# A 31st key/value slot in a one-core, two-layer cached-attention decode kernel

## The chip, the cores and the metric

The kernel runs on one core of a Trainium2 chip. The metric is the device time of one execution in microseconds; the time before is the median of three runs.

## What is computed

Eight sequences decode one token each through two identical layers; a layer is an attention block over a cache (A) and a mixer/MLP block (B), both with residuals. With one token per sequence the mixer's shifted parts fall away, so B is `x1 = x`, then `x1 + gelu(LN(x1) @ w3) @ w4`.

```python
def _A_ref(x, k_cache, v_cache, wq, wo):          # x (8, 1, 448), caches (8, 8, 4096, 256) bf16
    q = (x @ wq).reshape(B, 1, 16, 256)...
    k = jnp.repeat(k_cache, 2, axis=1)            # 16 query heads, 8 key/value heads
    v = jnp.repeat(v_cache, 2, axis=1)
    scores = jnp.einsum("bhqd,bhkd->bhqk", q, k) * (256 ** -0.5)
    o = jnp.einsum("bhqk,bhkd->bhqd", _softmax(scores), v)
    return o.reshape(B, 1, 4096) @ wo
...
x = x + _A_ref(_layernorm(x), A_k_cache, A_v_cache, A_wq, A_wo)
x = x + _B_ref(_layernorm(x), B_w1, B_w2, B_w3, B_w4)
x = x + _A_ref(...)                               # the same caches and weights again
x = x + _B_ref(...)
```

## The kernel before, in words

**Units of work.** A batch has 8 key/value heads, treated as four pairs m = 0..3. A head's 4096 x 256 keys (or values) are four chunks of 512 KB: 128 partitions x 2048 bf16, eight consecutive keys a partition. A chunk lies in one of `NSLOT = 30` slots of `SLOT = 2048` columns. One load brings one, two or four neighbouring slots (512, 1024 or 2048 KB); all loads are issued by SP (line 444), in one order fixed beforehand.

**Layers.** The batches run one after another, each with its layer-0 pairs, then a *turn*, then its layer-1 pairs. Layer 1 reads the same keys: those of pairs 1, 2 and 3 stay in slots in transposed form (24 chunks, of which three are *parked* as transposed tiles in PSUM and copied back by ACT, `unpark`, line 1100), and pair 0's keys are loaded again. V is loaded for both layers. In the stream, the loads of one pair's K alternate with those of the V of the pair before.

**Scores.** A chunk of K is transposed in one of two ways. The first `NN[m]` chunks of a head go whole through PE (128 x 128, line 819) into PSUM and are evicted by ACT into the same slot (line 878); their scores need the plain query (line 888, 16 matmuls a chunk). The others are transposed by DVE in 32 x 32 blocks into another free slot (line 900, two instructions a chunk, some 1.2 us each), and the raw slot comes free; their scores need the query spread into a block diagonal (`diagonal`, lines 623, 629, 635, kept in `qe`) and come from line 909, 16 matmuls a chunk as well.

**Softmax of a pair** (`kpart`): maximum over DVE (923) and POOL (925), subtraction (927), exponential by ACT into a tile `pE` (930), POOL's copy of the natural columns into `pN` (932), a PE transpose of `pE` (936), a DVE transpose into `pT` with zeros between the columns (938), then the sum (941), POOL's all-reduce (943) and the reciprocal (944). `pT` and `pN` have four buffers each; the zeros are written once at the start.

**P*V** (`vpart`): mostly with V moving, 128 x 512 (line 1002). The result in PSUM is split into two bf16 parts, the negated rounding by ACT (1012) and the remainder by DVE (1014), in a tile `half`, and eight small matmuls gather it (1023). The last pair before a turn has V as the stationary operand instead (974), which needs no such parts.

**The turn** (`turn`): output projection (1051), residual, norm, w3, gelu, w4 (592), norm, wq as rows (667), an ACT copy of the rows into `qe` (671), a transposition into columns (675), and the block diagonals of pairs 1, 2, 3 and 0.

**The planner** (`Plan.schedule`) runs when the program is built: every operation has an engine, a cost, dependences and a priority, and a list scheduler fixes the order on each engine and the slot of each load. An ACT or DVE operation that makes a chunk (an operation with a `target`) takes a free slot when it is placed. A load of four or two slots is cut in half when no such run of slots is free and the stream would run dry:

```python
if short and len(us) == 4 and transfer < t + DRY4:
    order.insert(nxt[0] + 1, self.split(u, users))
...
if (len(us) == 2 and short and transfer < t + DRY and one is not None and ...):
    order.insert(nxt[0] + 1, self.split(u, users))
```

## Time and profile before

| | |
|---|---|
| median of three runs | 1101.11 us (1100.97 to 1103.56) |
| the profiled execution | 1103.15 us, span 1101.3 us |
| busy: PE, PEld, DVE, ACT, POOL | 775.3, 534.9, 792.4, 223.4, 77.5 us |
| loads into slots | 361 (85 of 2 MB, 217 of 1 MB, 58 of 512 KB, one small) |

PE is TensorE's matmuls, PEld its weight loads, which overlap them; DVE is VectorE, ACT ScalarE, POOL GpSimd, SP SyncE, which only issues loads. A group's line gives line, engine, operation, tiles, shapes and count, then busy us and mean ns of one, then the idle time before them with what ended it. `A <- B` among the waits reads "A waited for B". A stretch's line gives its length, each engine's busy time (with the number of instructions), the granted TensorE clock, the DMA engines' share and GB/s.

### The profile page before, as it was taken

To read this page: it belongs to the slowest core of one execution; us is meant where nothing else is said; L and a number is where in the kernel's file an instruction comes from. 1 tells how busy PE (TensorE), PEld (TensorE's weight loads), DVE (VectorE), ACT (ScalarE), POOL (GpSimd) and SP (SyncE) were. 2 spreads that over 40 slices of the span, in tenths; PEclk is the share of its full clock that TensorE was granted. 3 is DMA by queue.
4 is the path that set the end of the run, shared out by engine and by line. 5 is a ranking of instruction groups with operands and counts; after the bars stand their busy time and mean duration, and the time that the engine had idled before them with its cause. 6 is when DMAs were issued, how large, how long until landed. Compare 5 with 4: busy or idle time off the path is not lost.

```text
span 1101.3 us, 33772 instructions
## 1 busy us (share of the span) xinstructions
PE 775.3 (70%) x15552; PEld 534.9 (49%) x15552; DVE 792.4 (72%) x1472; ACT 223.4 (20%) x313; POOL 77.5 (7%) x208
## 2 busy tenths in 40 slices
PE   2567588668757875778757787577776688676874
PEld 2355455354545563555525554354644456345553
DVE  4999549864897379955898558974689737995552
ACT  1022122112211131213202132121221113121310
POOL 0000001000100010000100000000010001000010
PEclk9999565565655555555655555555555555555555
DMA  9999999999999999999999999999999999999994
GB/s 342 406 421 405 395 392 423 423 394 410 425 425 408 412 425 427 423 397 415 424 427 420 399 420 427 426 418 405 414 427 423 406 408 423 428 422 395 420 425 182
DMA packets 59166, 448.96 MB, mean 408 GB/s; under 512 B 6016, under 2 KB 12048, under 8 KB 19984
## 3 DMA queue, kind: packets, MB, share of 16 engines
q1 hardware_dynamic: 59024, 446.80, 98.4%
q8 instruction: 122, 2.00, 0.7%
q14 instruction: 20, 0.16, 0.0%
HBM read 446.77 MB, written 0.01 MB: 406 GB/s over the span
## 4 chain that ended last, share of the span: by engine, by line
DMA 37%; DVE 28%; PE 20%; issue 7%; ACT 4%; POOL 1%; POOLq 0%; ACTq 0%; DVEq 0%; SPq 0%
DMA slot<-in_A_k_cache_dram 26%; DVE slot L900 18%; DMA slot<-in_A_v_cache_dram 11%; PE psV L1002 7%; PE psS L909 7%; ACT slot L1100 3%; PE psS L888 2%; DVE pT L938 1%; PE psT L592 1%; DVE half L1014 1%; PE psT L1051 1%; ACT half L1012 1%; DVE small L527 1%; PE psK L819 1%; POOL small L555 1%
## 5 line engine op out<-in xcount | busy, mean ns | idle before, releaser
L900 DVE STREAM_TRANSPOSE slot<-slot 128x1024 bf16<-128x1024 bf16 x512 | 602.5, 1220 | 49.1 <-DMA slot<-in_A_k_cache_dram 48.4
L909 PE MATMUL psS<-qe,slot 128*128 128x8 bf16 x6528 | 257.8, 175 | 164.5 <-DVE slot L900 140.5
L909 PEld LDWEIGHTS psS<-qe,slot 128*128 128x128 bf16 x6528 | 218.9, 105 | 291.9 <-DVE slot L900 236.3
L1002 PE MATMUL psV<-slot,pT 128*8 128x512 bf16 x1416 | 178.9, 582 | 6.6 <-DMA slot<-in_A_v_cache_dram 3.7
L878 ACT COPY slot<-psK 128x1024 bf16<-128x1024 bf16 x112 | 109.7, 1023 | 182.2 <-PE psK L819 182.2
L819 PE MATMUL psK<-ident,slot 128*128 128x128 bf16 x896 | 102.5, 302 | 15.3 <-DMA slot<-in_A_k_cache_dram 9.4
L1012 ACT ACTIVATE half<-psV 128x512 bf16<-128x512 f32 x55 | 33.0, 600 | 318.5 <-PE psV L1002 303.7
L819 PEld LDWEIGHTS psK<-ident,slot 128*128 128x128 bf16 x896 | 86.5, 140 | 20.3 <-DMA slot<-in_A_k_cache_dram 10.4
L1014 DVE TENSOR_TENSOR half<-psV,half 128x512 bf16<-128x512 f32 x55 | 37.3, 678 | 61.3 <-ACT half L1012 61.1
L925 POOL PARTITION_ALL_REDUCE small<-small x64 | 23.9, 374 | 699.0 <-DVE small L923 699.0
L938 DVE STREAM_TRANSPOSE pT<-psS 128x128 bf16<-128x128 bf16 x64 | 44.8, 701 | 8.8 <-PE psS L936 8.3
L1002 PE MATMUL psV<-slot,pN 128*8 128x512 bf16 x344 | 46.7, 553 | 2.9 <-DMA slot<-in_A_v_cache_dram 2.8
L930 ACT ACTIVATE pE<-psS 128x128 bf16<-128x128 f32 x64 | 18.3, 286 | 133.3 <-DVE psS L927 121.5
L977 DVE TENSOR_REDUCE small<-psV 128x8 f32<-128x32 f32 x9 | 1.7, 192 | 56.1 <-PE psV L974 56.1
L888 PE MATMUL psS<-small,slot 128*128 128x2 bf16 x896 | 31.4, 166 | 11.1 <-ACT slot L1100 6.4
L1002 PEld LDWEIGHTS psV<-slot,pT 128*8 128x8 bf16 x1416 | 25.9, 88 | 25.0 <-issue 11.0
L1051 PE MATMUL psT<-small,wo_sb 128*128 128x1 bf16 x1024 | 32.8, 165 | 7.4 <-DVE small L980 3.9
L888 PE MATMUL psS<-qo,slot 128*128 128x2 bf16 x768 | 27.9, 167 | 12.8 <-ACT slot L878 7.4
L974 PE MATMUL psV<-pT,slot 128*128 128x2 bf16 x864 | 28.8, 166 | 11.0 <-DMA slot<-in_A_v_cache_dram 10.9
L888 PEld LDWEIGHTS psS<-qo,slot 128*128 128x128 bf16 x768 | 24.0, 102 | 25.5 <-ACT slot L878 18.1
L888 PEld LDWEIGHTS psS<-small,slot 128*128 128x128 bf16 x896 | 28.1, 104 | 16.2 <-ACT slot L1100 8.5
L923 DVE TENSOR_REDUCE small<-psS 128x4 f32<-128x128 f32 x64 | 17.8, 278 | 23.8 <-PE psS L909 23.6
(156 smaller groups left out, 681.2 us busy)
## 6 DMA issues: line engine op xcount, KB each, us to landing
slot<-in_A_v_cache_dram SPq DMA_DIRECT2D x151, 1024.0 KB, 9.7
slot<-in_A_k_cache_dram SPq DMA_DIRECT2D x43, 2048.0 KB, 19.3
slot<-in_A_v_cache_dram SPq DMA_DIRECT2D x42, 2048.0 KB, 22.5
slot<-in_A_k_cache_dram SPq DMA_DIRECT2D x66, 1024.0 KB, 12.3
slot<-in_A_v_cache_dram SPq DMA_DIRECT2D x42, 512.0 KB, 6.6
slot<-in_A_k_cache_dram SPq DMA_DIRECT2D x16, 512.0 KB, 6.1
wo_sb<-in_A_wo_dram SPq DMA_DIRECT2D x4, 896.0 KB, 19.0
wq_sb<-in_A_wq_dram SPq DMA_DIRECT2D x3, 1024.0 KB, 9.5
```

Of the source, the lines that this page charges most:

```text
L819: last = e.transpose(tile[:, j * P:(j + 1) * P], slots[u.slot][:, o:o + P], ident[:, :])
L878: return e.copy(slots[u.slot][:, 1024 * t:1024 * t + 1024], tile)
L888: last = e.matmul(o, slots[u.slot][:, i:i + P], q, start=(cc == 0), stop=(cc == 1))
L900: return e.transpose(o, i)
L909: last = e.matmul(o, slots[u.slot][:, i:i + P], qe[:, 128 * pm_ + 64 * s + 8 * g:128 * pm_ + 64 * s + 8 * g + 8], start=(g == 0), stop=(g ...
L938: add("dve", lambda e: e.transpose(pT[y].rearrange("p (n u r) -> p n r u", u=3, r=4)[:, :, :, 0:3:2], psS[x][:, 128:192].bitcast(bf).rearr ...
L974: last = e.matmul(o, slots[u.slot][:, i:i + P], w, start=(j == 0), stop=(j == 7))
L1002: last = e.matmul(psV[x][32 * i:32 * i + 8, :].rearrange("p (k d) -> p k d", k=2), w, v, start=(s == 0 and c == 0), stop=(s == 1 and c == ...
L1012: add("act", lambda e: e.activation(part(0), psV[x][:, :], ACT.Copy, scale=-1.0), 590, [], [Bhalf[0]], [bV[x]], prio=at - 1, name=n + "ve0")
L1014: add("dve", lambda e: e.tensor_tensor(part(1), psV[x][:, :], part(0), ALU.add), 590, [Bhalf[0]], [Bhalf[1]], [bV[x]], prio=at - 1, name=n ...
L1051: last = e.matmul(psT[:, 4 * (2 * s + i) + c:4 * (2 * s + i) + c + 1], wo_sb[:, a, d0:d0 + P], o1[b % 2][:, a:a + 1], start=(k == 0), stop ...
L1100: E = add("act", lambda e, v=v, t=t, tile=tile: e.copy(slots[v.slot][:, 1024 * t:1024 * t + 1024], tile), 1045, [], [], [bank], [v], prio= ...
```

## The change

The SBUF of several small tiles is given up, and one more slot takes it.

- `NSLOT` goes from 30 to 31.
- The tile `half` is gone: the two bf16 parts of a P*V with V moving lie in a free slot, taken when ACT writes the first and released by the gathering matmuls. The rounding is no longer negated; DVE subtracts it instead.
- `qe` shrinks from four pairs' queries to a ring of two; `diagonal` makes one pair's at a time. In layer 1 those of pairs 1 and 2 are made in the turn, those of 3 and 0 when their scores are laid out. The small tiles of norm and gelu lie in `qe` too.
- The turn's rows of q (before in `qe`) go into the first half of the slot of a parked chunk, whose second half is copied back before them and whose first half after the columns are made.
- `pE` is gone: the exponential writes p into the pair's `pT`. When PE, DVE's sum and POOL's copies have read it, POOL zeroes the gaps, and DVE's transpose then fills the rest. The sum now comes before that transpose.
- `NP` and `NZ` go from 4 to 3; `pN` is one tile of three parts, of which the pair with two natural chunks takes two neighbouring ones. V of the pair before is laid out before the next K, so that its buffers return first.
- `NN` becomes one tuple per layer. In layer 1 only pair 3 has whole-transposed chunks: the reloaded pair 0 goes entirely through DVE, and the two chunks of pair 2 that layer 0 transposed whole are read by the block form's matmuls.
- The parked pieces are copied back in another order (`TS`, and the priorities in `unpark`).

```diff
-NSLOT = 30
+NSLOT = 31
-NP = 4
-NN = (1, 0, 1, 1)
-NZ = 4
+NP = 3
+NN = ((1, 0, 1, 1), (0, 0, 0, 1))
+NZ = 3
+TS = (1, 0)
...
-    qe = sb("qe", [P, 512], bf)
-    half = sb("half", [P, 1024], bf)
-    pE = sb("pE", [P, P], bf)
+    qe = sb("qe", [P, 256], bf)
     pT = [sb(f"pT{i}", [P, 192], bf) for i in range(NP)]
-    pN = [sb(f"pN{i}", [P, 96], bf) for i in range(NZ)]
+    pN = sb("pN", [P, 48 * NZ], bf)
...
+    def diagonal(layer, b, m):
+        k = nq[0] % 2
+        nq[0] += 1
...
-        add("act", lambda e: e.activation(qe[:, :], psT[:, :], ACT.Copy, scale=sf[:, 2:3]), 590, [Bs["f"]], Bqe, [bT], name=n + "qr")
+        v, Brow = kept[b, 3][1, 0], Buf()
+        E = unpark(b, 1, ready, [1], -1.0)
+        R = add("act", lambda e: e.activation(slots[v.slot][:, 0:512], psT[:, :], ACT.Copy, scale=sf[:, 2:3]), 590, [Bs["f"]], [Brow], [bT], [v], name=n + "qr")
...
+        C = add("pe", columns, 300, [Brow, Bc], [], [bT], [v], name=n + "qc", n=4)
+        unpark(b, 1, C, [0], -0.4)
+        diagonals[1, b, 1] = diagonal(1, b, 1)
+        dve(lambda e: e.tensor_copy(q2, psT[:, 88:96]), 180, [], [Bq2], [bT], name=n + "q2")
+        diagonals[1, b, 2] = diagonal(1, b, 2)
...
-        add("act", lambda e: e.activation(pE[:, :], xs, ACT.Exp, scale=INV_SQRT_DH), 300, [], [BpE], [bS[x]], prio=pr, name=n + "ex")
+        pE, pZ = pT[y][:, 0:128], pT[y].rearrange("p (n u r) -> p n u r", u=3, r=4)
+        add("act", lambda e: e.activation(pE, xs, ACT.Exp, scale=INV_SQRT_DH), 300, [], [BpT[y], BpZ[y]], [bS[x]], prio=pr, name=n + "ex")
...
+        add("dve", lambda e: e.tensor_reduce(rs, pE.rearrange("p (n k) -> p k n", k=4), axis=AX.X, op=ALU.add),
+            190, [BpZ[y]], [B_["pm"]], prio=pr, name=n + "rs")
+        plain = BpZ[y].readers[:]
+        Z = add("pool", lambda g: g.memset(pZ[:, :, 1], 0.0), 150, [], [BpZ[y]], prio=pr, name=n + "pz")
+        add("dve", lambda e: e.transpose(pZ[:, :, 0:3:2]..., psS[x][:, 128:192]...), 220, [], [BpT[y]], [bS[x]], prio=pr, name=n + "pq")
...
-            part = lambda i: half[:, 512 * i:512 * i + 512]
-            add("act", lambda e: e.activation(part(0), psV[x][:, :], ACT.Copy, scale=-1.0), 590, [], [Bhalf[0]], [bV[x]],
-                prio=at - 1, name=n + "ve0")
-            add("dve", lambda e: e.tensor_tensor(part(1), psV[x][:, :], part(0), ALU.add), 590, [Bhalf[0]], [Bhalf[1]], [bV[x]],
-                prio=at - 1, name=n + "ve1")
+            v, Bhalf = Unit(f"{n}H", None, 0), [Buf(), Buf()]
+            part = lambda i: slots[v.slot][:, 512 * i:512 * i + 512]
+            add("act", lambda e: e.activation(part(0), psV[x][:, :], ACT.Copy), 590, [], [Bhalf[0]], [bV[x]],
+                [v], prio=at - 1, name=n + "ve0").target = v
+            add("dve", lambda e: e.tensor_tensor(part(1), psV[x][:, :], part(0), ALU.subtract), 590, [Bhalf[0]], [Bhalf[1]], [bV[x]],
+                [v], prio=at - 1, name=n + "ve1")
...
         K(1, b, 1)
-        unpark(b, 2, parts[1, b, 1].scores[U2])
-        unpark(b, 0, parts[1, b, 1].scores[U0])
+        unpark(b, 2, parts[1, b, 1].scores[5], TS)
+        unpark(b, 0, parts[1, b, 1].scores[5])
         K(1, b, 2), K(1, b, 3)
+        weave(*K(1, b, 0, 4, (1, b, 1, False, 4)))
```

171 lines of the change are left out of this document (79 added, 92 removed).

## The prediction

> **What bounds the kernel now.** I read the page's head first (span, DMA), then who waits on SP's queue, then the span cut into stretches, and last the chain of waits around one turn.
>
> ```profile
> span 1101.3 us, 33772 instructions
> q1 hardware_dynamic: 59024, 446.80, 98.4%
> HBM read 446.77 MB, written 0.01 MB: 406 GB/s over the span
> ```
>
> The 16 DMA engines are busy for 98.4% of the span, and nothing in the change alters the 447 MB. So the time is bytes over rate, and I look for the places where the rate falls. Stretches of the trace (length, busy time of PE, PEld, DVE, ACT, POOL with instruction counts, granted clock, DMA share, GB/s); the first eight are the ten microseconds around each batch's turn, the others what lies behind them:
>
> ```profile
> 145.00:155.00 10.00, 8.74 (x169) 4.40 (x167) 4.07 (x22) 3.00 (x4) 0.38 (x1) 0.75 0.95 335
> 240.00:250.00 10.00, 7.66 (x201) 6.41 (x193) 3.84 (x9) 0.88 (x2) 1.12 (x3) 0.50 0.94 337
> 350.00:360.00 10.00, 7.61 (x193) 6.31 (x193) 5.08 (x10) 0.88 (x2) 1.12 (x3) 0.50 0.99 381
> 480.00:490.00 10.00, 6.88 (x169) 5.57 (x170) 6.39 (x11) 0.88 (x2) 1.12 (x3) 0.56 0.97 369
> 611.00:621.00 10.00, 6.64 (x160) 5.34 (x161) 6.63 (x11) 0.87 (x2) 1.12 (x3) 0.50 0.98 381
> 745.00:755.00 10.00, 7.10 (x195) 6.37 (x192) 3.40 (x9) 0.88 (x2) 1.12 (x3) 0.50 1.01 383
> 875.00:885.00 10.00, 7.69 (x193) 6.31 (x193) 4.97 (x10) 0.88 (x2) 1.12 (x3) 0.50 0.99 374
> 1005.00:1015.00 10.00, 6.99 (x173) 5.68 (x174) 6.27 (x11) 0.87 (x2) 1.12 (x3) 0.59 0.96 370
> 155.00:240.00 85.00, 61.12 (x1214) 42.95 (x1214) 69.15 (x94) 19.05 (x26) 6.46 (x17) 0.55 1.01 422
> 250.00:265.00 15.00, 12.16 (x225) 6.29 (x224) 7.22 (x47) 3.22 (x5) 0.79 (x2) 0.58 1.01 424
> 265.00:275.00 10.00, 9.04 (x195) 5.77 (x193) 3.82 (x12) 2.33 (x3) 0.38 (x1) 0.55 1.01 406
> 385.00:480.00 95.00, 66.68 (x1270) 46.62 (x1266) 81.43 (x107) 23.08 (x31) 7.58 (x20) 0.53 1.01 424
> ```
>
> Between turns the stream runs at 422 to 424 GB/s, whatever the engines do. Ahead of every turn it falls to 335 to 383, and just behind it to about 406. What the queue waits for (SP's own waits: total, times, longest), and the chain at 237:
>
> ```profile
> SPq L444 <- PE psS L909: 422.7, 122, 10.4
> SPq L444 <- PE psV L1002: 267.8, 82, 9.9
> SPq L444 <- PE psV L974: 53.6, 32, 6.7
> ```
>
> ```profile
> 236.97 4.63 DVE slot L900 x4
> 241.60 0.02 issue
> 241.62 7.76 DMA slot<-in_A_v_cache_dram
> 249.38 0.05 issue
> 249.42 0.60 PE psV L974 x16
> ```
>
> SP stands almost always at a load that lacks a free slot, freed by the last matmul that reads it (scores L909, P*V L1002 and L974). That is harmless while enough is in flight. Ahead of a turn it is not: 24 chunks of K are kept for layer 1 (three of them parked in PSUM), so 21 of 30 slots are shut, and V of pair 3 waits in the rest for the softmax of the last K. The last V load goes out only when DVE's last transposes release raw K (241.62), and the turn begins behind its landing. Slots, not an engine, set the dips.
>
> **What the change does, part by part.**
>
> *The 31st slot.* At 424 GB/s 2048 columns (524 KB) are 1.24 us of stream. The loss of a dip against 424 is 10 x (1 - rate/424): 2.10, 2.05, 1.01, 1.30, 1.01, 0.97, 1.18, 1.27, together 10.9 us. A slot repays at most 1.24 of each: 9.1 us. The order of the changed program bears this out: the planner cuts a load in half when no pair of slots is free, and the half-megabyte loads of V ahead of a turn fall from six to two, all those of K behind it go; in all 18 are left of these 58:
>
> ```profile
> slot<-in_A_v_cache_dram SPq DMA_DIRECT2D x42, 512.0 KB, 6.6
> slot<-in_A_k_cache_dram SPq DMA_DIRECT2D x16, 512.0 KB, 6.1
> ```
>
> *The bf16 parts in a slot.* Each of the 55 moving P*V now takes a slot from ACT's copy to the gathering matmuls. Just ahead of the turn at 240 (timeline):
>
> ```profile
> 240.79 0.60 ACT L1012 ACTIVATE half<-psV 128x512 bf16<-128x512 f32 x1 [4.92 <-PE psV L1002]
> 242.47 0.19 PE L1023 MATMUL psV<-same,half 128*128 128x4 bf16 x2
> ```
>
> 240.79 to 242.66 is 1.87 us of a ten-microsecond dip, so I keep 81% of 9.1: **7.4 us gained**. The ends are 0 (the slot is lent just when it is short) and 10.9 (all dips close). Elsewhere slots are plentiful. ACT's copy also waits now for a free slot; behind it on ACT stand the exponential of the next pair and the evictions, which nobody awaits in the streaming stretches.
>
> *Behind the turn.* Seven such stretches (the first is quoted above, the last here) average 404 GB/s, by the rows at 265, 376, 507, 638, 770, 901 and 1032.
>
> ```profile
> 1032.00:1042.00 10.00, 8.70 (x193) 5.41 (x194) 3.65 (x13) 2.01 (x4) 0.38 (x1) 0.60 1.02 412
> ```
>
> Against 424 that is some 3 us over seven turns, with K in two halves and one megabyte. With K in megabytes I take half: **1.6 us gained** (ends 0 and 3.3). Two V loads of the fill, at about 90 us, are newly halved: by the same row (406 for 424, two halves in it) 0.4 us lost.
>
> *p inside its tile.* The exponential writes into pT, and before DVE can put the transposed p there, POOL must zero the gaps and so wait for its own copy of p, PE's transpose and DVE's sum, which moves ahead of the transpose. The copy of one chunk, the sum, and the two nearest POOL memsets:
>
> ```profile
> L932 POOL COPY pN<-pE 128x32 bf16<-128x32 bf16 x56 | 18.0, 321 | 54.6 <-ACT pE L930 54.1
> L941 DVE TENSOR_REDUCE small<-pE 128x4 f32<-128x128 bf16 x64 | 19.8, 310 | 7.8 <-ACT pE L930 7.8
> L457 POOL MEMSET ident<- 128x128 bf16 x1 | 0.2, 204 | 0.3 <-POOLq L1289 0.3
> L1289 POOL MEMSET const-bfloat16-1.0<- 128x1 bf16 x1 | 0.1, 101 | 0.0
> ```
>
> 64 elements a partition lie between 101 and 204 ns; with two hand-overs I take 0.25 us a softmax. Copy and sum run beside PE's transpose. It counts only in the softmax ahead of each turn, where V's slots wait for p: 8 x 0.25 = **2.0 us lost**. The low end is 0, since chunk 0 goes through pN first and the last V lands only at 249.38. The high end is one 1.22 us transpose of K that slips in front on DVE at each turn: 9.8 us. POOL's all-reduce of the sums stands behind the memset; only the final scaling awaits it.
>
> *More for DVE, less for ACT and PE.* In layer 1 only pair 3 keeps the whole transposition, so the reloaded pair 0 goes entirely through DVE: 32 more big transposes (544 for 512) and 32 fewer evictions on ACT. The diagonals of q are made for one pair at a time: 64 spreads and 64 puts for 34 of each.
>
> ```profile
> L900 DVE STREAM_TRANSPOSE slot<-slot 128x1024 bf16<-128x1024 bf16 x512 | 602.5, 1220 | 49.1 <-DMA slot<-in_A_k_cache_dram 48.4
> L635 DVE TENSOR_TENSOR qe<-psT,small 128x128 bf16<-128x128 f32 x18 | 5.2, 288 | 7.3 <-PE psT L629 7.3
> L623 DVE TENSOR_TENSOR qe<-psT,small 128x32 bf16<-128x32 f32 x16 | 3.1, 191 | 7.4 <-PE psT L675 4.1 <-PE psT L629 3.4
> L878 ACT COPY slot<-psK 128x1024 bf16<-128x1024 bf16 x112 | 109.7, 1023 | 182.2 <-PE psK L819 182.2
> ```
>
> 32 x 1.22 = 39 us, and 30 more pairs of diagonals at 0.48 us are 14 us at most, since the larger ones they replace cost more: 53 us, 6.6 a batch. The stretch 385 to 480 has 95 - 81.4 = 13.6 us of DVE idle, in which this hides at **0 us**; ACT's 33 us saved hide too. If that cover is gone, the last K's transposes come late, and with them the turn (the slower rival).
>
> *In the turn.* The copy of q to rows now waits for one unparking copy on ACT instead of two, about 1 us sooner, and the second goes behind the columns; pair 3's and pair 0's diagonals leave the turn and wait for the ring's earlier pair, while PE scores the pair between. DMA runs at 424 through the turn (250 to 265), so this moves nothing: 0.
>
> *The memset of starting tiles, the smaller pools (three pT), the packed small tiles:* once or renamed, 0. Three pT suffice, since at most three pairs lie between exponential and P*V; pair 0's exponential in layer 1 now awaits P*V of the pair three before it, streamed with it.
>
> *The sum*: -7.4 - 1.6 + 0.4 + 2.0 = -6.6 us. The profiled execution took 1103.15 us (span 1101.3 and 1.85 around it) and would take 1096.5; it stood 2.0 us over the median of 1101.11, so the median goes to **1094.5**.
>
> **A rule weighed.** The row first: 250 to 265 carries loads of one megabyte and less at 424 GB/s, while each takes microseconds to land. The Trainium skill's "DMA: Bandwidth & Descriptors", section Anatomy of one DMA, gives a load a fixed cost of about 2.0 us beside its bytes, for the GpSimd path. The new program issues 28 fewer slot loads (333 for 361), so by that rule, taken serially, the time would be an estimated 56 us less, 1045. The trace disagrees: these costs overlap here, so I give that time no chance.
>
> **Rivals.** (a) *The slot buys nothing*: the parts borrow it at every dip. For it: the loan at 240 falls inside the dip. Against it: the loan ends 1.9 us later, and the order has fewer halves. Then -1.6 + 0.4 + 2.0 = +0.8: 1101.9. (b) *DVE's extra work is not absorbed.* The place is the backlog of K from behind the turn; it decides once DVE no longer stands idle for K before the last pair. For it: DVE has stretches without a gap already (DVE alone: length, busy, clock, DMA share, GB/s), and part of its idle time is spent waiting on PE and ACT. Against it: 13.6 us idle for 6.6 more, and DMA at 433 and 429 in these very rows.
>
> ```profile
> 300.00:305.00 5.00, 5.00 (x6) 0.50 1.03 433
> 305.00:310.00 5.00, 5.00 (x5) 0.50 1.01 429
> ```
>
>  If only half of the idle can be used, 6.8, it fits just; if a fifth can, 2.7, then 6.6 - 2.7 = 3.9 us a turn, over the seven turns that follow a reload 27 us, less the 6.6 gained: 1101.1 + 20.7 = 1122; at a third, 4.5, it is 2.1 x 7 - 6.6 = +8.1: 1109, which I take as its time. (c) *The dips close entirely* and p's longer chain hides: -10.9 - 3.3 = -14.2: 1087.
>
> **Chances.** Forecast 0.55, (a) 0.14, (b) 0.18, (c) 0.13. About 0.3% (3.3 us) is what a measurement here can tell from none. The forecast's own range, 1088 to 1100, reaches over that bound a little: 0.50 of its 0.55 is faster, 0.04 same and 0.01 slower. With (c) faster is 0.63; with (a) same is 0.18; with (b) slower is 0.19. The range reaches down to (c) and up past (a) into the near part of (b): 1086 to 1106.
>
> **What would show it.** Right: the ten microseconds ahead of each turn at 400 GB/s or more; a half-megabyte row of 18; the last V load issued a megabyte earlier against DVE's last transposes; DVE busy up to 53 us more and still with waits on K. Wrong: dips as deep as now (a); in the streaming stretches GB/s below 420 with DVE above 93% (b); a wait of DVE's pT transpose on POOL of a microsecond at each turn; ACT's copy of the parts waiting for a slot.

## The result and the profile after

The changed kernel takes 1099.26 us (median of 8 runs, 1098.01 to 1100.15) where the kernel before takes 1101.84 on the same chip (8 runs, 1100.55 to 1103.74): a ratio of 0.9975 [0.9964, 0.9986], so 2.6 us or 0.25% faster. The prediction was 6.6 us faster, 1094.5; the time lies inside its range, 1086 to 1106, and within the 0.3% that it called no difference. The profiled execution took 1099.27 us (before: 1103.15, which is 1.3 us over its own median; so times are compared below by medians and ratios, while all that is read from a trace is one execution of each kernel).

The head of the profile after, its queues and two groups:

```profile
span 1097.5 us, 33719 instructions
PE 760.9 (69%) x15416; PEld 521.1 (47%) x15416; DVE 831.1 (76%) x1556; ACT 195.0 (18%) x281; POOL 79.3 (7%) x256
q1 hardware_dynamic: 54992, 446.80, 98.4%
q8 instruction: 121, 1.98, 0.7%
...
L893 DVE STREAM_TRANSPOSE slot<-slot 128x1024 bf16<-128x1024 bf16 x544 | 648.7, 1228 | 37.6 <-DMA slot<-in_A_k_cache_dram 32.8
...
L939 DVE STREAM_TRANSPOSE pT<-psS 128x128 bf16<-128x128 bf16 x64 | 44.9, 702 | 4.3 <-PE psS L931 2.1
```

The loads of half a megabyte, as the DMA view of the profile after groups them:

```profile
slot<-in_A_v_cache_dram SPq DMA_DIRECT2D x16, 512.0 KB, 6.9
slot<-in_A_k_cache_dram SPq DMA_DIRECT2D x2, 512.0 KB, 7.0
```

Stretches of the profile after. The first eight stand at the same distance from each turn as the eight of the prediction; then two turns from their first step on, one stretch inside the turn at 491.47, one behind a turn, and the streaming stretch:

```profile
143.00:153.00 10.00, 9.32 (x174) 4.53 (x171) 4.22 (x22) 3.10 (x4) 0.38 (x1) 0.77 0.98 379
236.90:246.90 10.00, 6.84 (x197) 6.29 (x196) 3.55 (x10) 0.87 (x2) 1.24 (x4) 0.50 1.01 397
346.60:356.60 10.00, 7.19 (x180) 5.82 (x181) 4.56 (x9) 0.87 (x2) 1.24 (x4) 0.50 1.00 399
477.10:487.10 10.00, 6.36 (x162) 5.27 (x158) 5.43 (x10) 0.87 (x2) 1.24 (x4) 0.58 1.00 400
608.10:618.10 10.00, 7.25 (x181) 5.87 (x182) 5.69 (x10) 0.87 (x2) 1.24 (x4) 0.52 1.00 411
741.60:751.60 10.00, 6.84 (x193) 6.27 (x193) 3.46 (x9) 0.87 (x2) 1.24 (x4) 0.50 0.99 401
871.70:881.70 10.00, 7.00 (x178) 5.68 (x178) 4.24 (x9) 0.87 (x2) 1.24 (x4) 0.50 0.99 394
1001.70:1011.70 10.00, 7.39 (x177) 5.87 (x177) 4.76 (x10) 0.87 (x2) 1.24 (x4) 0.50 1.01 410
...
491.47:501.47 10.00, 8.54 (x164) 4.60 (x164) 5.91 (x43) 0.80 (x3) 0.79 (x2) 0.50 1.03 415
496.50:506.50 10.00, 9.43 (x167) 4.61 (x165) 4.10 (x22) 3.20 (x4) 0.40 (x1) 0.69 1.00 383
...
1016.10:1026.10 10.00, 8.54 (x164) 4.59 (x164) 5.91 (x43) 0.80 (x3) 0.79 (x2) 0.50 1.00 393
...
264.00:274.00 10.00, 9.07 (x255) 6.98 (x252) 5.06 (x11) 4.54 (x6) 0.94 (x3) 0.50 1.01 420
...
385.00:480.00 95.00, 63.70 (x1146) 42.27 (x1146) 86.38 (x115) 15.30 (x22) 6.80 (x22) 0.54 1.01 424
0.00:130.00 130.00, 69.66 (x1359) 53.37 (x1360) 103.66 (x162) 24.04 (x30) 8.22 (x30) 0.83 1.01 398
```

The same turn, and the same first 130 us, in the kernel before:

```profile
0.00:130.00 130.00, 70.00 (x1329) 52.80 (x1330) 103.92 (x164) 24.14 (x30) 7.55 (x24) 0.93 1.00 393
494.40:504.40 10.00, 9.01 (x168) 4.70 (x168) 5.96 (x43) 0.36 (x2) 0.79 (x2) 0.50 1.01 419
499.40:509.40 10.00, 8.40 (x128) 3.52 (x124) 4.00 (x22) 3.00 (x4) 0.40 (x1) 0.67 1.02 422
```

Ahead of the turns the picture is what was forecast. Counted as the prediction counted it, 10 x (1 - rate/424), the eight dips lose 1.06, 0.64, 0.59, 0.57, 0.31, 0.54, 0.71 and 0.33 us, together 4.7 where before they lost 10.9: 6.2 us less, against 7.4 predicted. Behind the turn 406 GB/s became 420; over the seven stretches of the prediction, taken at the same distance from each turn, the mean went from 404 to 417, a little more than forecast. But the time fell by 2.6 us, not by 8. Inside the turn, where the kernel before ran at 419 and 422, there is now a second dip, 383 in the turn at 491.47. And the first 130 us run at 398 for 393 GB/s, 130 x 5/424 = 1.5 us, which the prediction had put at 0.4 us lost.

### The profile page after: what moved, and what is told of

Its sections match the earlier page's. It is cut to its first block, busy times and chain, and to the rows that moved or that the text cites. A ratio compares the mean times of both kernels' runs of the same rounds, so it can differ in the third digit from the quotient of the medians.

```text
span 1097.5 us, 33719 instructions
## 1 busy us (share of the span) xinstructions
PE 760.9 (69%) x15416; PEld 521.1 (47%) x15416; DVE 831.1 (76%) x1556; ACT 195.0 (18%) x281; POOL 79.3 (7%) x256
## 4 chain that ended last, share of the span: by engine, by line
DMA 36%; DVE 32%; PE 21%; issue 7%; ACT 1%; POOL 0%; DVEq 0%; POOLq 0%
DMA slot<-in_A_k_cache_dram 26%; DVE slot L893 23%; DMA slot<-in_A_v_cache_dram 9%; PE psV L1005 7%; PE psS L902 5%; PE psT L656 2%; DVE pT L939 2%; DVE slot L1018 1%; PE psT L587 1%; PE psV L977 1%; PE psS L881 1%; PE psT L1054 1%; DVE qe L623 1%; DVE psS L920 1%; DVE small L916 1%
## 5 line engine op out<-in xcount | busy, mean ns | idle before, releaser
L893 DVE STREAM_TRANSPOSE slot<-slot 128x1024 bf16<-128x1024 bf16 x544 | 648.7, 1228 | 37.6 <-DMA slot<-in_A_k_cache_dram 32.8
L1005 PE MATMUL psV<-slot,pT 128*8 128x512 bf16 x1536 | 197.9, 587 | 7.6 <-DMA slot<-in_A_v_cache_dram 2.6
L871 ACT COPY slot<-psK 128x1024 bf16<-128x1024 bf16 x80 | 78.3, 1015 | 175.7 <-PE psK L810 175.6
L1016 ACT ACTIVATE slot<-psV 128x512 bf16<-128x512 f32 x55 | 33.2, 603 | 344.2 <-PE psV L1005 298.1
L810 PE MATMUL psK<-ident,slot 128*128 128x128 bf16 x640 | 74.6, 308 | 6.6 <-DMA slot<-in_A_k_cache_dram 6.5
L810 PEld LDWEIGHTS psK<-ident,slot 128*128 128x128 bf16 x640 | 63.8, 143 | 7.9 <-DMA slot<-in_A_k_cache_dram 7.4
L1018 DVE TENSOR_TENSOR slot<-psV,slot 128x512 bf16<-128x512 f32 x55 | 37.1, 675 | 11.5 <-ACT slot L1016 11.5
L925 ACT ACTIVATE pT<-psS 128x128 bf16<-128x128 f32 x64 | 18.0, 281 | 155.4 <-DVE psS L920 155.4
L1054 PEld LDWEIGHTS psT<-small,wo_sb 128*128 128x128 bf16 x1024 | 30.9, 104 | 6.9 <-DVE small L983 3.2
L977 PEld LDWEIGHTS psV<-pT,slot 128*128 128x128 bf16 x896 | 27.0, 105 | 14.2 <-DMA slot<-in_A_v_cache_dram 11.4
```

The source lines that it names most:

```text
L810: last = e.transpose(tile[:, j * P:(j + 1) * P], slots[u.slot][:, o:o + P], ident[:, :])
L871: return e.copy(slots[u.slot][:, 1024 * t:1024 * t + 1024], tile)
L893: return e.transpose(o, i)
L977: last = e.matmul(o, slots[u.slot][:, i:i + P], w, start=(j == 0), stop=(j == 7))
L1005: last = e.matmul(psV[x][32 * i:32 * i + 8, :].rearrange("p (k d) -> p k d", k=2), w, v, start=(s == 0 and c == 0), stop=(s == 1 and c == ...
L1016: add("act", lambda e: e.activation(part(0), psV[x][:, :], ACT.Copy), 590, [], [Bhalf[0]], [bV[x]], [v], prio=at - 1, name=n + "ve0").targ ...
```

## The experiments

The kernel before was timed beside each run and took 1100.7 to 1102.3 us, so each run is given as its median and as its ratio to the kernel before timed with it; 0.001 is 1.1 us. A ratio is uncertain by some 0.0011 either way, and a difference of two ratios by some 0.0016, which is 1.7 us; this has to be kept in mind with the small differences below. Five wo tiles are left out where a run needs the room: they aren't loaded, and the matmuls that need them read the last tile kept, so PE's work stays. Two numbers more stand beside each run, worked out from its one trace; turns are numbered from 0 to 7. *Dips* are the losses against 424 GB/s per turn (mean of turns 1 to 7) in the 15 us ahead of the turn's first step and from 5 to 20 us behind it. *Lateness* is taken from the loads alone, not from GB/s: the sum, from 30 us ahead of turn 2 to 30 us behind turn 7 (some 716 us), of how much later each load of K or V landed behind the one before than 1.2385 us a chunk of 512 KB, the pace of the undisturbed stream (the median in two36 from 130 us on). Kernels with the same time (after, early, behind) read 13.8, 12.0 and 11.6, so a difference of 2 us in this column decides nothing.

```
kernel      slots  what it is                              median   ratio  [95%]             dips        lateness
before      30                                             1101.8   1                        1.50 0.50   13.7
after       31     the change                              1099.3   0.9975 [0.9964, 0.9986]  0.98 0.85   13.8
cutb        30     before, 5 wo tiles out                  1099.7   0.9974 [0.9963, 0.9984]  1.22 0.55   13.5
slot31      31     before + slot, 5 wo tiles out           1096.5   0.9960 [0.9946, 0.9975]  0.70 1.05   12.3
own30       30     after, no loan, 5 wo tiles out          1099.6   0.9979 [0.9969, 0.9989]  1.38 0.43   14.2
own31       31     after, no loan, 5 wo tiles out          1096.1   0.9950 [0.9938, 0.9962]  0.66 0.90   11.8
cut31       31     after, 5 wo tiles out                   1096.4   0.9957 [0.9945, 0.9969]  1.01 0.74   12.4
after30     30     after                                   1106.2   1.0043 [1.0028, 1.0057]  1.33 1.26   17.0
cut32       32     after, 5 wo tiles out                   1095.2   0.9940 [0.9928, 0.9952]  0.90 0.35   11.1
single      31     after, turn's V in 512 KB loads         1106.7   1.0043 [1.0030, 1.0057]  1.40 0.70   17.6
dry4        31     after, 48 more 512 KB loads             1103.5   1.0016 [1.0006, 1.0025]  1.27 0.84   16.6
whole       31     after, no 512 KB loads                  1109.9   1.0063 [1.0047, 1.0079]  1.84 1.19   20.0
two31       31     after, 1 MB for some 2 MB loads         1099.4   0.9981 [0.9970, 0.9992]  1.00 0.75   13.8
early       31     after, a P*V ahead of w4                1099.0   0.9973 [0.9961, 0.9985]  1.17 0.49   12.0
short31     31     after, turn without gelu and w4         1096.7   0.9953 [0.9936, 0.9969]  1.09 0.29   10.6
behind      31     after, first P*V behind projection      1099.3   0.9980 [0.9966, 0.9995]  0.88 0.63   11.6
tail_both   31     behind + last V in halves               1099.5   0.9979 [0.9970, 0.9989]  0.98 0.68   12.3
cut34       34     after, 16 wo tiles out                  1091.7   0.9915 [0.9901, 0.9928]  0.66 0.71   11.3
cut36       36     after, 24 wo tiles out                  1089.2   0.9888 [0.9875, 0.9902]  0.17 1.18   11.2
two36       36     cut36, 1 MB for some 2 MB loads         1090.7   0.9901 [0.9887, 0.9914]  0.69 0.52   12.1
```

**What each part is worth.** The theory behind the prediction: the loan of a slot to the parts eats a fifth of what the slot brings. Rivals: the other edits eat it, or a slot only moves the dip. First the loan taken away, with its control and with the slot alone in the old code:

```diff
+    half = sb("half", [P, 1024], bf)                                     # own31
-    wo_sb = sb("wo_sb", [P, 32, D], bf)
+    wo_sb = sb("wo_sb", [P, 27, D], bf)                                  # own31, cut31, slot31
-            part = lambda i: slots[v.slot][:, 512 * i:512 * i + 512]
+            part = lambda i: half[:, 512 * i:512 * i + 512]              # own31
-NSLOT = 30
+NSLOT = 31                                                               # slot31, in the kernel before
```

> The changed kernel with its 31 slots, but with the two bf16 parts back in a tile of their own; for the room five of the 32 tiles of wo are left out (573 KB less to load, 1.35 us of the stream), as in its control cut31. Theory, the loan: in the turn the parts of the first P*V hold their slot for 5.5 us (ACT's copy 500.9 to the gathering matmuls 506.1 to 506.4 in one turn), because the gathering goes to the turn's own PSUM bank and stands behind the turn; SP waits 20.5 us in eight times for just that release. Without the loan 0.8 to 1.2 us a turn come back: 5 to 9 us below cut31. Rival 1, the other edits (32 more transposes on DVE, the gaps zeroed on POOL) took the gain: within 1.5 us of cut31. Rival 2, the turn is limited by when the kept keys come free, and a slot only moves the dip: within 2 us of cut31, and the dip inside the turn (12 to 20 us behind the turn's start) stays below 390 GB/s.

> The changed kernel with five of the 32 tiles of wo left out, and nothing else: the control of own31. All theories: 1.35 us below the changed kernel's 1099.3, so 1097.9.

> The kernel before with 31 slots and nothing else of the change; five of the 32 tiles of wo are left out for the room (1.35 us). The loan: nothing is lent, so the slot is worth what the prediction said before the loan, 7 to 11 us, with the 1.35 on top: 1090 to 1094. Rival 1 (the other edits eat it): the same 1090 to 1094, and well below cut31. Rival 2 (a slot only moves the dip): 2 to 4 us and the 1.35: 1096 to 1098.5.

Without the loan 1096.06, with it 1096.38: by the ratios 0.8 us, not clear of noise (1.9), where 5 to 9 were expected. So at 31 slots the loan costs little, and the theory falls. The slot alone, 1096.47, does as well as the whole change. The same with the slot taken back, and one more:

```diff
-NSLOT = 31
+NSLOT = 30                                                               # after30
-NSLOT = 31
+NSLOT = 32                                                               # cut32 (and wo_sb of 27 tiles)
```

> The changed kernel with 30 slots, all else as changed. The loan: the lent slot is now one of 30, so it falls behind the kernel before: 1104 to 1108. Rival 1: the other edits cost 4 to 6 us and the loan little: 1105 to 1108 too, but then slot31 and own31 differ by that. Rival 2: the slot is worth what the change gained, 2 to 4 us: 1101 to 1103.

> cut31 with a 32nd slot (five tiles of wo left out in both). The loan theory has fallen: own31 and cut31 differ by 0.3 us. Theory, the odd slot: in a turn 21 slots are kept, and loads go out two slots at a time into aligned pairs. The trace of the changed kernel shows slots 5 and 7, then 7 and 23, empty from 485 to 501 us while SP waits: eight of ten slots carry loads, as many as eight of nine before. A 32nd slot closes the pairs: 3 to 6 us below cut31's 1096.4. Rival, a slot only moves the dip, each one worth less: 0 to 2 us below.

In the new code, with the loan, the slot from 30 to 31 is worth 0.0068, 7.5 us, the next one only 0.0017, 1.9 us. To tell whether at 30 slots the loan or the other edits cost:

```diff
-NSLOT = 31
+NSLOT = 30                                                               # own30: own31 with 30 slots
-    wo_sb = sb("wo_sb", [P, 32, D], bf)
+    wo_sb = sb("wo_sb", [P, 27, D], bf)                                  # cutb: the only edit to the kernel before
```

> The changed kernel with 30 slots and the parts of P*V in a tile of their own (no loan of a slot; five tiles of wo left out to make room, 1.35 us of stream less). The changed kernel with 30 slots took 1106.2. Theory 'each slot is worth less than the one before': without the loan the 30 slots give the time of the kernel before less wo, 1099.5 to 1100.5, so that the loan costs some 5 us at 30 slots and next to nothing (0.3) at 31. Rival 'the other edits cost': p inside its tile, V laid out ahead of K and the ring of queries take 4 to 5 us whatever the slots; then it takes 1103 to 1105, and the 31st slot's own worth is 7 us, near the 7.4 of the prediction.

> The kernel before (30 slots) with nothing changed but five of the 32 tiles of wo left out (573 KB, 1.35 us of stream at 424 GB/s): the control for the two runs that made room in this way. By bytes alone it takes 1.35 us less than the kernel before, 1100.2. Then the 31st slot by itself, with no other edit (1096.5 with the same tiles left out), is worth 3.7 us, and the other edits without the loan (1099.6 at 30 slots with the same tiles left out) -0.6. Rival 'the tiles are worth more than their bytes': the changed kernel with and without them differs by 2.9 us (1099.3 and 1096.4); then it takes 1098.6, the slot by itself is worth 2.1, and the other edits cost 1.

The wo tiles alone give 2.9 us in the old code (0.9974) and 2.0 in the new (0.9975 to 0.9957), where their bytes are 1.35. With the first as the base, the other edits without loan and slot are worth 0.0005, +0.6 us (the prediction had them at +0.8: -1.6, +0.4 and +2.0); the slot without a loan is worth 1.5 us in the old code (0.9974 to 0.9960) and 3.2 in the new (0.9979 to 0.9950); the loan costs some 4 us at 30 slots (1.0043 against 0.9979 + 0.0026) and 0.8 at 31. So of the 7.5 us above the greater part is the loan's own price at 30 slots. Each of these is uncertain by 1.6 to 2.7 us, so neither the other edits nor the loan at 31 slots can be told from nothing. The term that was forecast as 9.1 us is 1.5 to 3.2, and at most some 5.

**Is it the odd slot, or the halved loads?** With 31 slots one has no neighbour, and pairs might leave slots idle:

```diff
-            weave(V(1, b - 1, 2 + m, STILL[m], 2, not m) if b else V(0, AHEAD[m], 0, STILL[m], 2, not m))
+            weave(V(1, b - 1, 2 + m, STILL[m], 1, not m) if b else V(0, AHEAD[m], 0, STILL[m], 1, not m))   # single
-DRY = 2500.0
+DRY = 4000.0                                                             # dry4
-DRY = 2500.0
+DRY = -1e9                                                               # whole
```

> The changed kernel, with the two V's of each turn loaded in single slots (512 KB) instead of pairs: 116 more small loads. Packets of 4 KB take 159 ns at the median and those of 8 KB 309, so each small load costs 36 ns of stream, 4.2 us in all. The odd slot: every free slot can take a load, the dips go (1 to 1.2 us a turn), 2 to 5 us below the changed kernel's 1099.3 after the 4.2. Rival, slots are not short but come back late (V waits for P*V in PE's fixed order): 2 to 4.5 us above it.

> The changed kernel, in which the planner cuts a load in two already when the stream has 4 us left instead of 2.5: 48 more small loads, only where no pair is free. Price 48 x 36 ns = 1.7 us. The odd slot: 1 to 4 us below the changed kernel. Slots that come back late: 1 to 2 us above it.

> The changed kernel with no load cut from two slots to one: the 18 loads of 512 KB become nine of 1 MB (two at every turn, two in the fill), and nothing else is changed. All work is kept. Theory 'small loads cost by themselves': 48 more of them cost 4.2 us and 116 more 7.5, some 0.07 to 0.09 us each; 18 fewer give 1.2 to 1.6 us, 1097.7 to 1098. Rival 'the cut keeps the stream fed': in the turn at 491.47 the two halves are issued at -9.17 and -7.95 us, as one slot after the other comes free; as one load both go at about -8, the stream stands up to half a megabyte, 1.2 us, longer at each turn, and the time rises by up to 8 us, to 1100 to 1107; a wider dip between 15 and 0 us ahead of the turn's start (0.98 us a turn now) would show it.

More small loads cost 7.5 and 4.2 us by the medians, and none at all costs 10.6 (9.7 by the ratios): the eighteen halves that were left are worth more than any other part here. The lateness rises too (17.6, 16.6 and 20.0 for 13.8), so a good part of this is true stalls of the stream. By the rule weighed in the prediction (the Trainium skill, "DMA: Bandwidth & Descriptors", Anatomy of one DMA, some 2.0 us for each load on the GpSimd path; the loads here are issued by SP) nine loads fewer would give an estimated 18 us less; the run with nine fewer took 10.6 more.

**Do slots come back late?** In the turn at 491.47 the third V load landed 3.93 us behind the first step and was read at 6.78, behind w4; before the change it had landed at 5.15 and was read at 6.84. So it was tried to read it sooner, and to shorten the turn:

```diff
+    by = {o.name: o for o in plan.ops}                                   # early
+    for b in range(B):
+        n = f"B{b - 1}m2" if b else f"A{AHEAD[0]}m0"
+        for c in (0, 1):
+            by[f"turn{b}w4"].deps[by[n + f"V1{c}"]] = False
...
-        gelu(1, lambda: shf[:, :], lambda: sht[:, :], 16, [], n, 150, ...)      # short31
-        down(1, lambda: sht[:, :], 32, [], n + "w4")
-        dve(lambda e: e.scalar_tensor_tensor(x[:, 0:4], psT[:, 32:36], 0.5, sxy[:, :], ALU.mult, ALU.add), 150,
-            [Bs["xy"]], [Bx[b]], [bT], name=n + "r2")
+        dve(lambda e: e.tensor_copy(x[:, 0:4], sxy[:, :]), 150, [Bs["xy"]], [Bx[b]], name=n + "r2")
```

> The changed kernel with one constraint more: on PE, the P*V of the third load of V in a turn (two chunks) stands ahead of the turn's w4 instead of behind it. All work is kept. In the trace of the changed kernel, counted from the first step of the turn at 491.47, that load lands at 3.93 us and is read at 6.78, behind w4 (6.24), and the load that takes its slots is issued at 7.53; before the change it landed at 5.15 and was read at the same 6.84. Averaged over turns 1 to 7, the stream loses against 424 GB/s 0.98 us in the 15 us ahead of the turn's start (1.50 before the change) and 0.85 us between 5 and 20 us behind it (0.50 before). Theory 'slots come back late': the extra slot brings V earlier, but its readers keep their place between the turn's steps, so the slots return no sooner and the dip moves behind the turn's start. Then here the next load is issued about 2 us sooner, the second dip falls to 0.5 us or less, the first stays at 1.0, and the time falls by some 2 to 3 us, to 1096 to 1097.5. Rival 'the turn pays': w4 is put off by up to 1 us by the P*V, the scores of layer 1 by as much, and the time rises by 1 to 5 us. Rival 'only the number of slots counts': nothing moves by more than 1 us.

> The changed kernel with a shorter turn: the gelu and w4 of layer 0 are left out (x after the mixer is x1 plus its normalised part only), some 2.4 us of the chain between the turn's start and the scores of layer 1. The bytes are the same. Theory 'slots come back late': P*V of the turn is read 2 to 3 us sooner, the dip between 5 and 20 us behind the turn's start (0.85 us a turn) goes nearly away, and the time falls by 4 to 7 us, to 1092 to 1095. Rival 'only the number of slots counts': what ran dry ahead of the turn is not touched by the turn's length, and the second dip comes from the eight slots' own latency; the time falls by 1 us or less. Rival 'DVE': the turn holds back DVE's backlog of K; a turn shorter by 2.4 us gives back that much in each of the eight turns but only where DVE is late, so that GB/s between turns would rise: 5 us or more with no change of the dips.

In the first, the load behind went out at 4.76 instead of 7.53 and the second dip fell from 0.85 to 0.49, as the theory said; the time stayed (1098.99). The shorter turn took the second dip to 0.29 and gave 2.6 us, under the 4 to 7 expected; its trace shows the turn's second norm 2.5 us sooner behind the first step (4.0 for 6.5), but the first scores of layer 1 only 1.4 us sooner (mean 12.1 for 13.5). So slots that come back late do make the dip inside the turn, and it is worth little. Next, what puts off the turn itself: from the landing of its last V to its first step the trace shows 2.37 us with 30 slots and 3.29 on average with 31.

```diff
+        by[(f"B{b - 1}m2" if b else f"A{AHEAD[0]}m0") + "V00"].deps[by[f"W{b}m31"]] = False      # behind, tail_both
...
-            if len(group) == most:
+            if len(group) == most and not (last and i + most == NCH):    # tail_both: last V ahead of a turn in halves
```

> The changed kernel with one constraint more: on PE, the first P*V with V moving of a turn stands behind the output projection of the last pair instead of ahead of it. Loads and work are the same. From the landing of the last V before a turn to the turn's first step the traces show 2.37 us in every kernel with 30 slots (the last V comes as two loads of 512 KB, and the first moving P*V is read behind the projection), 2.80 with the last V as one load of 1 MB and that P*V still behind (the runs with no halved load and with 32 slots), and 3.1 to 3.8, mean 3.29, in the changed kernel, where 1 MB and a P*V ahead of the projection meet. Theory 'the slot's gain is given back ahead of the turn': the earlier V and the larger load put off the turn by 0.86 us. Then here the interval is 2.80, the turn starts 0.5 us earlier against the stream, and the time falls by 1 to 4 us (8 x 0.49), to 1095.5 to 1098. Rival 'it moves on': the slot of that V comes back 1.5 us later, so the next load goes out later and the dip around the turn's start grows by as much; the time stays within 1 us.

> As the run before (the first moving P*V behind the projection), and the last V ahead of each turn in two loads of 512 KB instead of one of 1 MB, as the kernel before had it. All work is kept. Theory: the interval from the last V's landing to the turn is 2.37 us as with 30 slots, 0.92 less than in the changed kernel, and the time falls by 2 to 7 us, to 1092 to 1097. Rival 'it moves on': within 1 us of the changed kernel. Rival 'small loads cost': 8 more halved loads give 0.7 us back (48 cost 4.2).

The interval went to 2.84 and 2.65 us, and the time stayed at 1099.28 and 1099.53; "it moves on" holds. Four edits had now moved or shrunk a dip in GB/s, and three of them left the time where it was.

**Are the dips a matter of slots at all?** Three and five slots more, room made by leaving out tiles of wo:

```diff
-    wo_sb = sb("wo_sb", [P, 32, D], bf)
+    wo_sb = sb("wo_sb", [P, 16, D], bf)      # cut34; cut36: 8 tiles
-NSLOT = 31
+NSLOT = 34                                   # cut36: 36
-            weave(*K(1, b, 0, 4, (1, b, 1, False, 4)))
+            weave(*K(1, b, 0, 2, (1, b, 1, False, 2)))     # two36 (on cut36) and two31 (on the change)
```

> The changed kernel with 34 slots; to make room, 16 of the 32 tiles of wo are left out (1.84 MB, 4.3 us of stream). By bytes alone the changed kernel would take 1095.0. From 35 us ahead of a turn's start to 50 us behind it the stream loses against 424 GB/s, a turn: 2.0 us with 31 slots, 1.6 with 32 (with five tiles left out), 2.8 with 30 and the loan. Theory 'slots still set the dips, each worth 0.3 to 0.4 us a turn': about 1.0 us a turn with 34, and 1086 to 1089. Rival 'the chain from the last K to the last V of the turn sets what is left': that chain is 34.4 to 35.5 us in all kernels so far; the loss stays at 1.4 us or more, 1091 to 1094. Rival 'each slot is worth its 1.24 us': the loss is gone, under 0.3 us, 1082 to 1084.

> The changed kernel with 36 slots; to make room, 24 of the 32 tiles of wo are left out (2.75 MB, 6.5 us of stream). By bytes alone 1092.8. Theory 'each slot 0.3 to 0.4 us a turn': the loss is 0.2 to 0.5 us a turn, 1080 to 1083. Rival 'the chain': 1.4 us a turn or more, 1088 to 1092. Rival 'each slot is worth its 1.24 us': no loss, 1079 to 1081, and no better than 34 slots but for the bytes (2.2 us).

> The run with 36 slots (16 tiles of wo and more left out as there), with one edit: behind a turn, the reloaded K of pair 0 and the V of pair 1 come in loads of 1 MB instead of 2 MB. With 36 slots the dip ahead of the turn was gone (0.17 us of loss in those 15 us, 0.98 with 31), but 0.88 us were lost from 15 to 20 us behind the turn's start: at the turn at 490 a load of 2 MB stood from 9.5 to 15.2 us, until the first scores of layer 1 had freed four neighbouring slots. Theory 'what the slots give ahead of the turn is taken back by the next load that waits for layer 1's scores': with 1 MB loads the first goes out as V of the turn returns its pairs, the dip at 15 to 20 falls to 0.3 us or less, the loss a turn from 1.42 to 0.8, and the time by 3 to 5 us, to 1084 to 1086. Rival 'it moves on': the loss comes back further behind, the time stays within 1 us of 1089.2.

> The changed kernel with the same edit alone (1 MB loads for the reloaded K of pair 0 and V of pair 1), all work kept. With 31 slots the first of these loads are halved already, so 26 more loads of 1 MB take the place of 13 of 2 MB. In the traces of this case 0.1 us or less is lost from 15 us behind the turn's start on. Expected: no gain, 1099 to 1100; a rival by which larger loads wait for runs of four here too gives 1096 to 1098.

Beyond the bytes left out, three slots more give 3.2 us and five more 3.6 (2.3 and 3.1 by the ratios), and some of either may be the tiles themselves. "Each slot is worth its 1.24 us" is refuted, "0.3 to 0.4 us a turn" as well. The rival "the chain" gave both times, 1091 to 1094 and 1088 to 1092, but no run shortened that chain, so it isn't shown to be the cause. Stretches of cut36 (its turn begins at 483.1): ahead of the turn nothing is lost any more, behind it 387 GB/s.

```profile
467.00:477.00 10.00, 6.08 (x135) 4.62 (x132) 6.87 (x11) 0.87 (x2) 1.21 (x4) 0.67 1.02 424
468.00:483.00 15.00, 9.75 (x253) 8.10 (x253) 7.25 (x14) 0.87 (x2) 1.21 (x4) 0.58 1.02 422
488.00:503.00 15.00, 13.69 (x291) 7.80 (x288) 4.98 (x26) 6.79 (x8) 0.77 (x2) 0.79 0.96 387
```

In two36 smaller loads took that dip away (0.52 for 1.18 us), and one ahead of the turn was there again (0.69 for 0.17); the time did not fall by the 3 to 5 us expected, it rose by 1.5. In two31 the smaller loads changed nothing, as expected.

**What the dip is.** The dip of the kernel before at 480 to 490, 369 GB/s, was priced at 1.30 us lost. But no load is late in it. These are the landings of K and V around it in that trace, how long behind the one before each came (loads of 1 MB up to 486.91 and from 496.97 on, between them 512 KB), and, in chunks of 512 KB, the bytes of all packets that had ended by then less those of the landed loads of K and V. Each figure of that last row holds 20.15 chunks of weights and x, which had landed long before, so the lead itself goes from 2.4 chunks to 1.0:

```
landed at us     479.49 481.97 484.59 486.91 488.19 489.47 490.74 492.00 493.24 494.48 496.97 499.52
since the last     2.48   2.48   2.62   2.32   1.28   1.28   1.27   1.26   1.24   1.24   2.49   2.55
chunks ahead      22.53  22.32  21.87  21.52  21.55  21.56  21.53  21.43  21.24  21.21  21.22  21.18
```

One megabyte lands every 2.48 us, straight through the dip: from 479.49 to 494.48 twelve chunks in 14.99 us, 1.25 each. What goes down is the lead of the engines that had run on, by 1.3 chunks, or 1.6 us of stream. The dip at 875 to 885 (374 GB/s) reads the same: landings every 2.46 to 2.49 us for a megabyte and 1.23 to 1.29 for a half, and the lead goes from 22.28 to 21.36. A load is done when the last of the 16 engines has done its part: for the one landed at 484.59 the trace has 16 updates of its semaphore, the first at 479.91. The engines that are ahead lose nothing for the kernel when they run short. Over all eight dips of the prediction, each with 3 us behind it, the loads land 2.4 us late together, where 10.9 were priced; in the two deepest, 335 and 337 GB/s, 0.6 and 0.4. Where the lead came from can be seen best in two36, where ten or more chunks were on their way at each late load. Its stretches ahead of the turn at 484.5 and from it on:

```profile
472.00:482.00 10.00, 7.30 (x185) 5.92 (x182) 4.25 (x9) 0.87 (x2) 1.21 (x4) 0.50 0.97 373
484.50:494.50 10.00, 9.22 (x168) 4.77 (x168) 5.92 (x44) 0.75 (x3) 0.79 (x2) 0.50 1.01 420
```

Here, too, the loads land every 2.46 to 2.51 us through the dip while the lead falls by 1.0 chunk; but at 459.41 a load had come 1.32 us late, and the lead had risen by 0.96 with it. Such steps of 1.2 to 1.4 us are nearly all that this kernel loses against the undisturbed pace, and each stands at an instruction fetch (packets of the queue q8, 16 KB, about 1.07 us each, one every 6 to 17.5 us). Numbered from 0, from 130 us on:

```
fetch          16    24    32    40    48    56    64    72    80    88    96   104   112
at us         169   245   311   378   455   517   598   658   743   803   883   950  1025
load late by 1.18  1.20  1.24  1.27  1.32  1.38  1.42  1.36  1.41  1.35  1.38  1.27  1.31
```

It is every eighth, without exception, and beyond these there are three gaps of 0.31 to 0.35 us. In cut34 the late landings of more than 0.3 us stand at the same thirteen fetches, 1.35 to 1.61 us each, and nowhere else. It isn't a place in the batch either: in two36 these fetches lie anywhere from 58 us ahead of the nearest turn to 58 us behind it. In the kernel before a step is often split, but of the 22 late landings of more than 0.3 us from 30 us ahead of turn 2 to 30 us behind turn 7, together 14.7 us, 18 with 12.5 us stand at fetches whose number leaves 0, 4 or 5 when divided by eight; 4 and 5 were found in this same trace, and in the changed kernel the late landings spread over more remainders, so with 30 and 31 slots the link is weaker. If the fetches came to the DMA engines in turn, and to the same engine again at every eighth, that would explain it; the trace does not name the engine of a packet, and no run changed the number of fetches by much (short31 has 117), so this cause is read from the trace and not shown by an experiment. The page of the kernel before has the row:

```profile
q8 instruction: 122, 2.00, 0.7%
```

The thirteen steps of two36 are 17.1 us of its span, more than the dips were thought to cost, and 36 slots do not remove them. What slots can touch is the rest of the lateness: 13.7 us before, 11.2 with 36 slots, so some 2.5 us over the six turns, little more than this column can tell.

## Why the prediction missed

**The slot, -9.1 us, is the step that failed.** It rested on two sentences: that the loss of a dip against 424 GB/s is time, and that a slot repays 1.24 us of each. The first is what failed. The dips did narrow, by 6.2 us of the prediction's own measure, 3.7 of them in turns 2 to 7, for which its sum would be 0.81 x 6.65 = 5.4 us. The lateness of the loads in these six turns did not move (13.7, then 13.8): what had narrowed was the time in which engines ahead of the slowest gave back their lead. The landings that show it are in the trace of before, and the prediction read only GB/s. Around turn 1 the lateness fell from 2.8 to 1.6, but it is 1.2 in cutb too, which has 30 slots. Measured, the slot is worth 1.5 to 3.2 us. About 1.5 of that is in the first 130 us, for the old code with the slot alone as for the change:

```profile
0.00:130.00 130.00, 70.84 (x1378) 53.42 (x1378) 104.14 (x164) 24.25 (x30) 7.56 (x24) 0.81 1.01 399
```

```profile
0.00:130.00 130.00, 71.14 (x1358) 53.73 (x1359) 103.82 (x164) 24.15 (x30) 7.54 (x24) 0.80 1.00 393
```

(slot31 above, cutb below: 1.8 us). In the old code it is paid once there, and not eight times: from the first turn's start to the eighth's the traces show 879.6 us before, 877.1 in cutb, 877.3 in slot31, 878.4 after. In the new code without the loan the turns do give something, 879.2 in own30 and 876.7 in own31, which is 2.5 us over seven turns and not 1.24 at each.

**"Slots, not an engine, set the dips"** was right for the place and wrong for the price. The turn's length does not set the time either: scores 1.4 us sooner at each of eight turns gave 2.6 us in all, and the change itself had already brought the first scores of layer 1 1.5 us nearer to the turn's first step (mean 13.5 for 15.1). Below what the stream needs slots do decide, as at 30 slots with the loan (17.0 us late) or without halves (20.0).

**The loan, 81%.** The 1.7 us that it took off were near the measured 0.8 by chance. It is no share of a slot: at 30 slots the loan costs some 4 us, at 31 some 0.8, not clear of nothing. In sum the other edits cost some 0.6 us, the slot brings 1.5 to 3.2, the loan takes up to 0.8, which leaves -0.1 to -2.6; measured -2.6. That the time fell inside the stated range is owed to the range, which reached up to rival (a), and not to the mechanism.

**Behind the turn, -1.6 us.** The rate there rose as forecast (420 for 406), but what holds for the dips holds here: the lateness does not show it. **The fill** was counted at 0.4 us lost for two halved loads; it gained 1.5. The gain lies between 80 and 100 us, at 416 GB/s (419 in slot31) for 397 before (387 in cutb). It isn't a chunk for each slot: with 36 slots, and less of wo to load, the first 130 us run no faster than in slot31:

```profile
0.00:130.00 130.00, 70.27 (x1473) 54.82 (x1474) 103.28 (x164) 24.30 (x30) 8.21 (x30) 0.81 1.00 399
```

**p inside its tile, +2.0 us,** did not show. The maximum, the sum and DVE's transposition into pT ahead of the turn at 494 before and at 491 after:

```profile
484.64 0.28 DVE L923 TENSOR_REDUCE small<-psS 128x4 f32<-128x128 f32 x1
486.06 0.29 DVE L941 TENSOR_REDUCE small<-pE 128x4 f32<-128x128 bf16 x1 [0.34 <-ACT pE L930]
486.65 0.72 DVE L938 STREAM_TRANSPOSE pT<-psS 128x128 bf16<-128x128 bf16 x1 [0.31 <-PE psS L936]
```

```profile
480.77 0.29 DVE L916 TENSOR_REDUCE small<-psS 128x4 f32<-128x128 f32 x1 [0.47 <-PE psS L902]
482.33 0.28 DVE L933 TENSOR_REDUCE small<-pT 128x4 f32<-128x128 bf16 x1
482.74 0.73 DVE L939 STREAM_TRANSPOSE pT<-psS 128x128 bf16<-128x128 bf16 x1
```

From the maximum to the transposition 2.01 us before, 1.97 after, and the same within 0.1 us at seven of the eight turns (0.25 more at turn 1). The step that was thought to cost it isn't in the program: DVE's transposition waits for those that read p, but not for POOL's zeroing, which writes other columns and starts beside it (482.75; POOL's times are rough). Only P*V needs both. In the whole trace the transposition waits for POOL once, 0.2 us for a copy of p. The low end of the range, 0, was the value.

**DVE's extra work, 0 us,** was right: 831.1 us for 792.4, 38.7 more of at most 53, at 424 GB/s in the streaming stretch with 86.4 of its 95 us busy. It still waits 32.8 us for K. Rival (b) is refuted; rival (c), closed dips, came with cut36 and did not bring its time; rival (a), a slot that buys nothing, came nearest, though not for the loan that it named. Of the signs that were listed, the 18 halves came exactly, the last V ahead of the turn at 491 goes out 12.6 us ahead of its first step instead of 10.2, and four of the eight dips are at 400 GB/s or more, the others at 379 to 399. One sign of being wrong came as well: ACT's copy of the parts waited for one of DVE's transpositions seven times, 39.6 us in all, where it had waited once before (14.8 us); by own31 the whole loan costs some 0.8 us. Most of the signs for the forecast held, then, and the time did not follow: none of them was a sign of time.

## What to carry to other kernels

Before a dip in GB/s is priced, look whether the loads in it land late: the rate is a sum over 16 engines, a load is done when the slowest has done its part, and the two can tell different stories for tens of microseconds. A buffer more paid its size once here, where the stream first ran short; at a dip that comes back every round it pays only as far as the loads there were truly late, and a run with several buffers more measures that limit. Give a sign of the *time* among what would show a step right, such as the period from one turn to the next, not only signs that the edit does what it says.

## What was not expected of the hardware

A stream with ten or more chunks of 512 KB on their way lost 1.2 to 1.4 us at every eighth instruction fetch from 130 us on (13 of 13 in two36, and 1.35 to 1.61 us at the same 13 in cut34). Nine loads fewer made the kernel 10.6 us slower, 48 more small ones 4.2. The wo tiles left out gave 2.0 to 2.9 us for 1.35 us of bytes; why is open. Open is also why engines that run ahead come to a halt near a turn even with 36 slots, and what a program with fewer instructions would gain; that was not tried.
